# Weight sums of a two-level product: accumulating DMAs replaced by adds on GpSimd

## The chip, the cores and the metric

One core of a Trainium2 chip runs the whole program. The metric is the time of one execution on the device in microseconds (us). The kernel before takes 921.2 us (median of three executions, 921.12 to 921.84).

## What is computed

The reference chains three stages over 2304 tokens (4 batches of 576, model width 512).

```python
# 1. attention with exponential features (8 heads of 64)
proj = x @ w_phi; proj -= max(abs(proj)); phi = [exp(proj), exp(-proj)]
num = phi(q) @ (phi(k).T @ v);  den = phi(q) @ sum(phi(k));  x = num / (den + 1e-6)
# 2. mixture of 8 experts, each token to its best one
out[mask_e] = gate * (relu(x[mask_e] @ w1[e]) @ w2[e])
# 3. feed-forward
h = x @ w_in;  out = (h * sigmoid(h)) @ w_out        # w_in [512, 2048], w_out [2048, 512]
```

The weights `w_in` and `w_out` of stage 3 arrive as 64-bit floats, seen as pairs of 32-bit words; the kernel turns them into 32-bit floats itself.

## The kernel before, in words

**Precision.** TensorE multiplies in a reduced 32-bit format. To keep 32-bit accuracy nearly every operand x is split into a high part (a cast on ScalarE, ACT) and a low part (x minus the high part, on VectorE, DVE), and a product is three matmuls, high by high, low by high, high by low (`three`, lines 798 to 801).

**Three stretches.** Attention runs to about 230 us. From there to about 528 us come 22 expert "slots" of 128 tokens each, `for s in range(1, NSF + 1)` from line 1428. From 528 to 712 us run 32 "units" (`unit`, line 1112) that form h = x @ w_in, and after that w_out is applied (`down`, line 1176).

**A slot.** In the loop body for s, the first product of slot s (`mm1(s, k)`, k = 0 to 3) runs first, then the second product of slot s - 1 (`mm2(s - 1, i)`, i = 0 to 3). Behind each of these eight steps stand the splits of weights that are needed later (`split`, lines 848 and 849), the steps of the routing, and a call `convert(s, n)` with n = 0 to 7. `xturn` and `hturn` turn the inputs of the two products; their low parts `xl` and `hl` are made at line 856. The low part `hl` is the last thing that a second product waits for. PE, ACT, DVE, POOL (GpSimd) and SyncE (SP) each execute their instructions in the order in which this code writes them; in the units and after them POOL's own order is left to the framework.

**A unit.** Stage 3's first product is a seven-product scheme in place of eight: each pair q of 128-column blocks of w_in (eight pairs) gives seven weight matrices of 128x256. `unit(u)` goes through the products in the order 1, 5, 4, 6, 3, 2, 7, where 4 and 3 belong to the unit before; a plan `todo` hangs other work behind (unit, product). `keep` (line 1097, ACT) copies a partial sum from bank A out to an `ht` tile, `join` (line 1104, DVE) adds bank C or B to such a tile. Products 1, 6, 7, 4 accumulate in bank A, so each of them waits for the `keep` of the one before it; product 3 accumulates on product 5 in bank C, so it waits for the `join` of product 5. Products 1, 5, 2 of unit 0 and 1, 5 of unit 1 run ahead of the units, among the last slot's work.

**The seven weights.** A converted block holds two matrices of 128x256 (even block: A11 and A12, negated; odd block: A21, A22). The seven weights are these four, with one of them used alone in each place, and four sums. They are collected in HBM scratch, `sscr[q]`, seven places of 128x256. `keep_weights` (line 171) writes the four matrices, some of them to several places at once, and `add_weights` (line 191) then adds place n onto other places with a DMA that accumulates, HBM to HBM, issued by POOL. There are 21 such DMAs; `ADDS` and `WHEN` (lines 188, 189) put them into the slots, at the top of slot s, behind the gather of token rows for slot s + 2 (`gather`, line 834).

**Conversion.** Blocks 0 to 9 are converted on DVE during attention (`Convert`). Blocks 10 to 15 are converted in the slots (`cload`, `cwork`, `cstore`, lines 939 to 954): POOL issues the load of 512 KB, and `narrow` (line 197) takes four steps, one on ACT (line 202) and three on DVE (lines 209 or 212, 217, 219), in two raw buffers and one shared result buffer; an odd block also has one add on DVE (line 225). `HOOKS` (line 956) gives each block five places, the blocks lying in slots 4 to 8 and 13 to 16.

**Fetching.** `wfetch(q)` (line 984, SP) loads the seven places of pair q, 896 KB, straight into the buffer where the low parts will stand; `whigh` (line 990, ACT) casts them to the high parts, `wlow` (line 994, DVE) subtracts in place. Fetches of pairs 0 to 3 stand in slots 20 and 21, of 4 and 5 ahead of unit 0, of 6 and 7 in units 1 and 2. The 16 blocks of w_out are converted later, in units 6 to 24 (`oload`, `cwork`, `cstore`).

Of the kernel before, what the change touches and what calls it, by code (L numbers as in the profile page):

```python
# [49 lines left out]
RANK = (1, 0)  # L50
WARM = (10, 14)
# [15 lines left out]
def moe_kernel(ctx, tc, qk, v, w_phi, emb, tau, w1, w2, win, wout, out):  # L67
# [11 lines left out]
    sscr = [dram.tile([P, 7, 256], F32, name=f"sscr{i}") for i in range(NJP)]  # L79
# [91 lines left out]
    def keep_weights(i, c, rw, dma=nc.sync):  # L171
# [3 lines left out]
        if half:  # L175
            dma.dma_start(out=woscr[q][:, odd, :], in_=c)
        elif i < CA and odd:
            dma.dma_start(out=sscr[q][:, 6, :], in_=c[:, 0:256])
            dma.dma_start(out=sscr[q][:, 2:6, :], in_=c[:, 256:512].unsqueeze(1).to_broadcast([P, 4, 256]))
        elif odd:  # L180
            both = rw.rearrange("p f t -> p (f t)")[:, 0:256].bitcast(F32)
            dma.dma_start(out=sscr[q][:, 6, :], in_=c[:, 0:256])
# [5 lines left out]
    ADDS = [(q, n) for n in (6, 0, 1) for q in range(CA // 2)] + [(5, 0), (6, 0), (5, 1), (6, 1), (7, 0), (7, 1)]  # L188
    WHEN = [1, 1, 2, 2, 4, 6, 6, 6, 7, 7, 8, 13, 13, 13, 13, 14, 15, 15, 16, 17, 18]

    def add_weights(q, n):
        a, b = {6: (3, 6), 0: (4, 7), 1: (5, 6)}[n]
        src = sscr[q][:, n:n + 1, :]
        nc.gpsimd.dma_start(out=sscr[q][:, a:b, :], in_=src.to_broadcast([P, b - a, 256]) if b - a > 1 else src,
                            accum_op=ALU.add)

    def narrow(rw, c, eng, i):
        minus = i < NJ and i % 2 == 0
        lo, hi = rw[:, :, 0], rw[:, :, 1]
        def scale():  # L200
            if eng is nc.scalar:
                nc.scalar.mul(out=c.bitcast(F32), in_=hi.bitcast(F32), mul=2.0 ** -112)
            else:
                eng.tensor_scalar(out=c.bitcast(F32), in0=hi.bitcast(F32), scalar1=2.0 ** -112, scalar2=None,
                                  op0=ALU.mult)

# [20 lines left out]
    class Convert:  # L227
# [18 lines left out]
        def store(self, i):  # L246
            keep_weights(i, *self.h.pop(i))
# [1375 lines left out]
```

## Time and profile before

| | |
|---|---|
| median of 3 executions | 921.2 us (921.12 to 921.84) |
| profiled execution, its own time | 923.77 us |
| its span, first to last instruction | 922.1 us |
| granted TensorE clock in it | 0.998 of full speed |
| busy: PE, DVE, ACT, POOL | 901.1, 619.6, 581.9, 260.6 us |
| DMA in all | 171.69 MB; POOL's queue 26.55 MB of it |

The profile is of one execution; the sum of a prediction is made against its own time. PE is TensorE's matmuls; the end of a matmul is modelled, so two that follow each other overlap in the profile and a busy PE need not be at its peak. "Idle before <-X" names what released the instruction, by the profile. A group of instructions is named by its line of the kernel, its output and its inputs.

### The profile page before, as it was taken

The page shows a single profiled execution, that of the slowest core. Times are in us where ns is not written, and L with a number is a line of the kernel's source. Part 1 is how long each engine was busy: PE and PEld are TensorE (multiplying, and loading weights), DVE is VectorE, ACT ScalarE, POOL GpSimd, SP SyncE. Part 2 cuts the span into 40 slices and gives each one's busy share as a digit, 9 for nine tenths or more (in the row PEclk, how much of TensorE's full clock was granted, in tenths as well). Part 3 has the DMA queues.
Part 4 walks back from the last instruction along what each step waited for, and adds up shares of the span by engine and source line. Part 5 has one row for each costly group of instructions (what it writes and reads, how often), then busy time and mean ns, then how long its engine had stood idle before and what let it go on. Part 6 is the DMA issues. An engine that isn't in the chain of part 4 may idle for free. (4 is left out here: it accounts for less than half of the span.)

```text
span 922.1 us, 15645 instructions
## 1 busy us (share of the span) xinstructions
PE 901.1 (98%) x5567; PEld 786.3 (85%) x5567; DVE 619.6 (67%) x967; ACT 581.9 (63%) x948; POOL 260.6 (28%) x236
## 2 busy tenths in 40 slices
PE   8999999999999989999999999999999999999996
PEld 6999999988767767877888799999999888888885
DVE  7888888986798999969989857676756122222220
ACT  6877878745977869869888665343456344444331
POOL 6887877712221434313210020101000100000000
PEclk9999999999999999999999999999999999999999
DMA  6355363349496795793698585877776744444420
GB/s 181 107 152 180 93 178 97 99 126 359 160 256 194 237 240 170 277 322 110 180 335 305 196 289 180 248 248 231 242 255 210 202 115 125 115 114 115 116 67 23
DMA packets 136739, 171.69 MB, mean 186 GB/s; under 512 B 34664, under 2 KB 97768, under 8 KB 136656
## 3 DMA queue, kind: packets, MB, share of 16 engines
q1 hardware_dynamic: 124064, 144.06, 49.4%
q0 software_dynamic: 12512, 26.55, 10.8%
q8 instruction: 45, 0.74, 0.3%
q14 instruction: 38, 0.31, 0.1%
q10 hardware_dynamic: 80, 0.03, 0.0%
HBM read 170.87 MB, written 52.04 MB: 242 GB/s over the span
## 5 line engine op out<-in xcount | busy, mean ns | idle before, releaser
L849 DVE TENSOR_TENSOR wl<-raw,wh 128x1024 fp32r<-128x1024 f32 (+1 forms) x166 | 187.6, 1173 | 28.1 <-ACT wh L848 22.6
L848 ACT CAST wh<-raw 128x1024 fp32r<-128x1024 f32 (+1 forms) x166 | 161.2, 1033 | 22.2 <-PE ph L801 10.8
L1173 DVE TENSOR_TENSOR hlt<-gt,hlt 128x1024 fp32r<-128x1024 f32 x34 | 41.7, 1226 | 146.4 <-ACT hlt L1172 146.4
L1097 ACT COPY ht<-puA 128x288 f32<-128x288 f32 x128 | 50.9, 400 | 91.9 <-PE puA L801 78.9
L800 PE MATMUL po<-wob,hlt 128*128 128x512 f32 x272 | 108.6, 399 | 0.0
L799 PE MATMUL po<-wob,hlt 128*128 128x512 f32 x272 | 107.2, 394 | 0.0
L801 PE MATMUL po<-wob,hlt 128*128 128x512 f32 x272 | 106.6, 392 | 0.0
L435 POOL TENSOR_TENSOR kl<-ke,kh 128x640 fp32r<-128x640 f32 x52 | 84.0, 1636 | 31.0 <-issue 23.1
L1193 ACT COPY os<-po 128x512 f32<-128x512 f32 x17 | 10.0, 587 | 108.0 <-PE po L801 108.0
L485 PE MATMUL pnx<-kv,qp 128*128 128x73 f32 x640 | 76.6, 275 | 0.0
L485 PEld LDWEIGHTS pnx<-kv,qp 128*128 128x128 f32 x640 | 74.1, 192 | 0.1
L1194 POOL DMA_INDIRECT out<-os,oidx x18 | 17.5, 974 | 179.1 <-ACT os L1193 168.6
L799 PE MATMUL ph<-wh,xh 128*128 128x512 f32 x166 | 67.1, 404 | 0.0
L801 PE MATMUL ph<-wh,xl 128*128 128x512 f32 x166 | 65.3, 394 | 0.9 <-DVE xl L856 0.9
L800 PE MATMUL ph<-wl,xh 128*128 128x512 f32 x166 | 64.8, 390 | 0.0
L396 DVE TENSOR_REDUCE m<-pqk 128x10 f32<-128x1280 f32 x32 | 47.5, 1486 | 24.5 <-PE pqk L390 24.5
L1104 DVE TENSOR_TENSOR ht<-puC,ht 128x288 f32<-128x288 f32 x64 | 29.1, 454 | 51.4 <-PE puC L801 44.6
L799 PEld LDWEIGHTS po<-wob,hlt 128*128 128x128 f32 x272 | 51.1, 188 | 13.1
L420 ACT ACTIVATE ke<-d 128x640 f32<-128x640 f32 x52 | 38.3, 737 | 37.0 <-DVE d L397 37.0
L801 PEld LDWEIGHTS po<-wob,hlt 128*128 128x128 f32 x272 | 51.1, 188 | 12.3
L800 PEld LDWEIGHTS po<-wob,hlt 128*128 128x128 f32 x272 | 51.1, 188 | 11.8
L390 PE MATMUL pqk<-wbd,zh 128*128 128x256 f32 (+1 forms) x320 | 59.5, 285 | 0.8 <-DVE d L397 0.6
(403 smaller groups left out, 2438.3 us busy)
## 6 DMA issues: line engine op xcount, KB each, us to landing
raw<-w SPq DMA_DIRECT2D x44, 1536.0 KB
raw<-w SPq DMA_DIRECT2D x44, 512.0 KB
hd<-ht SPq DMA_DIRECT2D x124, 144.0 KB
gt<-hd SPq DMA_DIRECT2D x15, 1024.0 KB
z<-qk SPq DMA_DIRECT2D x32, 288.0 KB
wo<-wout SPq DMA_DIRECT2D x16, 512.0 KB
yd<-ys SPq DMA_DIRECT2D x23, 256.0 KB
raw<-win SPq DMA_DIRECT2D x10, 512.0 KB
```

What stands on the lines that cost most here:

```text
L390: nc.tensor.matmul(out=pqk[0:r, c * 256:(c + 1) * 256], lhsT=z[:, c * P:c * P + r], rhs=wbd[:, j].rearrange("p h f -> p (h f)"), start=(i ...
L396: nc.vector.tensor_reduce(out=m, in_=pv, axis=AX.X, op=ALU.max, apply_absolute_value=True)
L420: nc.scalar.activation(out=ke, in_=kd, func=AF.Exp, scale=1.0 - 2.0 * s)
L435: nc.gpsimd.tensor_tensor(out=kl[:, :, s, :], in0=st.pop(("ke", g, s)), in1=kh[:, :, s, :].bitcast(F32), op=ALU.subtract)
L485: nc.tensor.matmul(out=pn[:, c, 0:73], lhsT=qp[:, s, c * P:(c + 1) * P], rhs=kv[:, s, 0:73], start=(s == 0), stop=(s == 1))
L799: nc.tensor.matmul(out=o, lhsT=ah, rhs=bh, start=first, stop=False, skip_group_check=more)
L800: nc.tensor.matmul(out=o, lhsT=ah, rhs=bl, start=False, stop=False, skip_group_check=more)
L801: nc.tensor.matmul(out=o, lhsT=al, rhs=bh, start=False, stop=last, skip_group_check=more)
L848: nc.scalar.copy(out=hi[:, 0:n], in_=sl[:, 0:n])
L849: nc.vector.tensor_tensor(out=lo[:, 0:n], in0=sl[:, 0:n], in1=hi[:, 0:n].bitcast(F32), op=ALU.subtract)
L1097: nc.scalar.copy(out=htile(u, at), in_=BK[u, "A"])
L1173: nc.vector.tensor_tensor(out=lo, in0=g, in1=hi.bitcast(F32), op=ALU.subtract)
```

## The change

Pairs 0 to 2 are now converted in the slots, in place (`narrow_in_place`), and POOL forms their four sums right there (`csum`), in the parts of the raw buffers that the conversion has freed; `cstore` writes seven places. Pairs 3 to 7 are converted during attention and stored as four places; each is fetched into a staging tile (two of them in turn), POOL forms the four sums in the tile (`wsum`), and `whigh` and `wlow` read it from there. The places of conversion steps, of some unit tasks (`xscale`, `xsum` of T4, `wlow` of pair 2), of the `join` of product 5 and of the conversion of w_out move too.

```diff
-    def keep_weights(i, c, rw, dma=nc.sync):
+    def keep_weights(i, c, dma=nc.sync):
...
         elif odd:
-            both = rw.rearrange("p f t -> p (f t)")[:, 0:256].bitcast(F32)
-            dma.dma_start(out=sscr[q][:, 6, :], in_=c[:, 0:256])
-            dma.dma_start(out=sscr[q][:, 2, :], in_=c[:, 256:512])
-            dma.dma_start(out=sscr[q][:, 3:6, :], in_=both.unsqueeze(1).to_broadcast([P, 3, 256]))
+            dma.dma_start(out=sscr[q][:, 0, :], in_=c[:, 0:256])
+            dma.dma_start(out=sscr[q][:, 3, :], in_=c[:, 256:512])
         else:
-            dma.dma_start(out=sscr[q][:, 0:2, :], in_=c.rearrange("p (a f) -> p a f", a=2))
-    def add_weights(q, n):
...
+            dma.dma_start(out=sscr[q][:, 1:3, :], in_=c.rearrange("p (a f) -> p a f", a=2))
+    def narrow_in_place(flat, i):
+        rw = flat.rearrange("p (f t) -> p f t", t=2)
+        lo, hi = rw[:, :, 0], rw[:, :, 1]
+        shift(lo, i)
+        yield
+        nc.vector.scalar_tensor_tensor(out=lo, in0=hi, scalar=-2147483648, in1=lo, op0=ALU.bitwise_and,
+                                       op1=ALU.bitwise_xor)
+        yield
+        nc.scalar.mul(out=hi.bitcast(F32), in_=hi.bitcast(F32), mul=2.0 ** -112)
+        yield
+        c = flat[:, 0:512]
+        nc.vector.scalar_tensor_tensor(out=c, in0=hi, scalar=3, in1=lo, op0=ALU.logical_shift_left, op1=ALU.bitwise_or)
...
+        def csum(q):
+            a, b = J[2 * q][0], J[2 * q + 1][0]
+            a11, a12, s1, s2, a21, a22, s4, s3 = (x[:, o:o + 256] for x in (a, b) for o in range(0, 1024, 256))
+            for o, x, y in ((s1, a22, a21), (s3, a11, a21), (s2, s1, a11), (s4, s2, a12)):
+                nc.gpsimd.tensor_tensor(out=o, in0=x, in1=y, op=ALU.add)
+
+        def cstore(q):
+            for i, o, at in ((0, 0, 0), (0, 512, 3), (1, 512, 5)):
+                nc.gpsimd.dma_start(out=sscr[q][:, at:at + 2, :],
+                                    in_=J[2 * q + i][0][:, o:o + 512].rearrange("p (a f) -> p a f", a=2))
+            nc.gpsimd.dma_start(out=sscr[q][:, 2, :], in_=J[2 * q + 1][0][:, 256:512])
+
+        SLOTWORK = {(5, 7): (csum, 0), (6, 1): (cstore, 0), (7, 1): (cload, 2), (7, 3): (cload, 3),
+                    (11, 1): (csum, 1), (13, 1): (cstore, 1), (13, 5): (cload, 4), (13, 7): (cload, 5),
+                    (16, 1): (csum, 2), (16, 3): (cstore, 2)}
+        STEPS = [(2, 1), (2, 3), (2, 5), (2, 7), (4, 1), (4, 5), (5, 1), (5, 5)]
+        STEPS += [(s, n) for s in (9, 10, 14, 15) for n in (1, 3, 5, 7)]
...
+            else:
+                W["r", q] = pools["ul"].tile([P, 2048], F32, tag="ws", name="ws", bufs=2)
+                nc.sync.dma_start(out=W["r", q][:, 0:1024], in_=sscr[q].rearrange("p a f -> p (a f)"))
+
+        def wsum(q):
+            r = W["r", q].rearrange("p (a f) -> p a f", a=8)
+            for o, a, b in ((4, 3, 0), (7, 1, 0), (5, 4, 1), (6, 5, 2)):
+                nc.gpsimd.tensor_tensor(out=r[:, o], in0=r[:, a], in1=r[:, b], op=ALU.add)
...
-                if n == 5 and v >= 0:
+                if n == 1 and v >= 0:
                     join(v, 5)
...
             if s < NSF:
                 if s + 2 < NSF:
                     gather(s + 2)
-                for i, when in enumerate(WHEN):
-                    if when == s:
-                        add_weights(*ADDS[i])
...
             if s == NSF - 1:
                 xfetch(1, 0)
                 xfetch(1, 1)
-                wfetch(3)
...
+        wfetch(3)
+        wfetch(4)
...
-            for q in range(2, NJP):
-                at(q - 2, 6, whigh, q)
-                at(q - 1, 5, wlow, q)
-            at(1, 4, wfetch, 6)
-            at(2, 4, wfetch, 7)
+            for q, steps in {2: (None, None, (0, 6), (0, 3)), 3: (None, (0, 7), (1, 6), (2, 1)),
+                             4: (None, (1, 2), (2, 6), (3, 1)), 5: ((2, 5), (3, 1), (3, 7), (4, 5)),
+                             6: ((3, 6), (4, 4), (4, 7), (5, 5)), 7: ((4, 3), (5, 4), (5, 7), (6, 5))}.items():
+                for f, when in zip((wfetch, wsum, whigh, wlow), steps):
+                    if when:
+                        at(*when, f, q)
+            at(0, 2, xscale, 1, 0)
+            at(1, 2, xscale, 1, 1)
...
-                at(u + 6, 2, xsum, k, "T4")
+                at(u + 7, 1, xsum, k, "T4")
...
-            units = [u for u in range(6, 25) if u not in (7, 15, 23)]
+            units = [u for u in range(8, 26) if u not in (15, 23)]
```

## Rows read from the trace of the kernel before

**Rows 1.** The page, busy time, share of the span and instructions of each engine.

```profile
PE 901.1 (98%) x5567; PEld 786.3 (85%) x5567; DVE 619.6 (67%) x967; ACT 581.9 (63%) x948; POOL 260.6 (28%) x236
```

**Rows 2.** PE's waits, whole run: who waited for whom, us, times, longest.

```profile
PE po L801 <- DVE hl L856: 3.0, 3, 1.3
PE py L801 <- DVE hl L856: 1.8, 1, 1.8
PE puA L799 <- ACT ht L1097: 1.3, 2, 0.8
...
PE puC L799 <- DVE ht L1104: 0.6, 1, 0.6
```

**Rows 3.** Windows by stretch: length, busy us of each engine, clock, DMA share, GB/s.

```profile
323.00:353.00 30.00, 26.85 (x145) 20.91 (x144) 28.43 (x42) 21.07 (x32) 9.56 (x11) 1.00 0.88 221
...
402.00:416.00 14.00, 13.78 (x68) 10.77 (x67) 7.26 (x10) 8.11 (x14) 0.00 (x0) 1.00 0.88 289
416.00:429.00 13.00, 12.55 (x60) 9.81 (x59) 13.00 (x16) 13.00 (x19) 2.09 (x3) 1.00 0.30 98
```

**Rows 4.** PE's timeline at two waits: start, length, instruction [idle before <-releaser].

```profile
331.96 0.50 PE L801 MATMUL py<-wh,hl 128*128 128x512 f32 x1 [1.77 <-DVE hl L856]
...
346.41 0.51 PE L801 MATMUL po<-wh,hl 128*128 128x512 f32 x1 [1.33 <-DVE hl L856]
```

**Rows 5.** DVE's conversion steps in the slots: busy us, mean ns, idle before.

```profile
L217 DVE SCALAR_TENSOR_TENSOR x<-x 128x512 int32<-128x512 int32 x6 | 5.0, 826 | 0.0
...
L209 DVE TENSOR_SCALAR x<-x 128x512 int32<-128x512 int32 x3 | 1.3, 427 | 0.0
L225 DVE TENSOR_TENSOR x<-x 128x256 f32<-128x256 f32 x3 | 1.3, 424 | 0.0
```

**Rows 6.** ACT's timeline, two long idles in the slots.

```profile
341.69 0.66 ACT L202 ACTIVATE x<-x 128x512 f32<-128x512 f32 x1 [4.21 <-DMA sscr<-x]
...
407.89 0.62 ACT L848 CAST wh<-raw 128x512 fp32r<-128x512 f32 x1 [6.20 <-PE ph L801]
```

**Rows 7.** Accumulating DMAs from 380 to 402 us: issue ns, starts, issue to landing.

```profile
L194 POOL DMA_DIRECT2D sscr<-sscr x5: 1012/1410/1841, 385.4 to 398.0; - x5
...
DMA to landing us min/median/max: 8.1/10.4/11.6
```

**Rows 8.** DVE during attention: ns min/median/max of two lines.

```profile
L219 DVE SCALAR_TENSOR_TENSOR raw<-raw x10: 693/2062/2074, 29.9 to 192.0; 128x512 int32<-128x512 int32 x10
...
L397 DVE TENSOR_TENSOR d<-pqk,m x32: 1491/1492/1493, 9.7 to 220.2; 128x1280 f32<-128x1280 f32 x32
```

**Rows 9.** POOL's smallest two-input operation on 32-bit floats: busy us, mean ns.

```profile
L412 POOL TENSOR_TENSOR vl<-ve,vh 128x320 fp32r<-128x320 f32 x24 | 21.3, 887 | 0.9 <-ACT vh L409 0.9
```

**Rows 10.** ACT's timeline at the first units: pair 2's cast, then two copies.

```profile
530.41 1.69 ACT L990 CAST wb<-wb 128x1792 fp32r<-128x1792 f32 x1
532.00 0.70 ACT L1097 COPY ht<-puA 128x288 f32<-128x288 f32 x2
```

**Rows 11.** DVE's timeline there: pair 2's low part, a join, a scaling of tokens.

```profile
532.81 2.02 DVE L994 TENSOR_TENSOR wb<-wb 128x1792 fp32r<-128x1792 f32 x1
...
536.02 0.46 DVE L1104 TENSOR_TENSOR ht<-puB,ht 128x288 f32<-128x288 f32 x1 [0.41 <-PE puB L801]
536.40 0.48 DVE L1014 TENSOR_SCALAR yt<-yt,gate_s 128x512 f32<-128x512 f32 x1
```

**Rows 12.** PE's timeline there: first matmuls of product 3, unit 0, and of the next.

```profile
534.15 0.30 PE L799 MATMUL puC<-xcB,wb 128*128 128x288 f32 x1
...
534.95 0.30 PE L799 MATMUL puB<-xcB,wb 128*128 128x288 f32 x1
```

**Rows 13.** The DMA queue's timeline on SP: the fetch of pair 4.

```profile
528.96 0.47 SPq L987 DMA_DIRECT2D wbr<-sscr  x1
```

**Rows 14.** The chain of waits: start, us; a 512 KB load on SP's queue, a matmul.

```profile
602.69 5.17 DMA wo<-wout
...
712.16 0.23 PE po L799
```

More of the change, by code (lines that the diff above doesn't have):

```diff
@@ L78, in moe_kernel @@
     yd = dram.tile([NT + 2 * P, DM], F32, name="yd")
-    sscr = [dram.tile([P, 7, 256], F32, name=f"sscr{i}") for i in range(NJP)]
+    sscr = [dram.tile([P, 7 if i < QD else 4, 256], F32, name=f"sscr{i}") for i in range(NJP)]
     woscr = [dram.tile([P, 2, DM], F32, name=f"woscr{i}") for i in range(NJP)]
@@ L188, in moe_kernel @@
-    ADDS = [(q, n) for n in (6, 0, 1) for q in range(CA // 2)] + [(5, 0), (6, 0), (5, 1), (6, 1), (7, 0), (7, 1)]
-    WHEN = [1, 1, 2, 2, 4, 6, 6, 6, 7, 7, 8, 13, 13, 13, 13, 14, 15, 15, 16, 17, 18]
-    def add_weights(q, n):
[L192 to L198, printed above, removed]
-        lo, hi = rw[:, :, 0], rw[:, :, 1]
[L200 to L205, printed above, removed]
-        def shift():
-            if minus:
-                nc.vector.tensor_scalar(out=lo, in0=lo, scalar1=29, scalar2=-2147483648, op0=ALU.logical_shift_right,
-                                        op1=ALU.bitwise_or)
-            else:
-                nc.vector.tensor_scalar(out=lo, in0=lo, scalar1=29, scalar2=None, op0=ALU.logical_shift_right)
-        for f in (shift, scale) if eng is nc.scalar else (scale, shift):
-            f()
-            yield
@@ L972, in phase_all, with owork, ostore @@
+        def owork(j):
+            next(J[NJ + j][1], None)
+        def ostore(j):
+            keep_weights(NJ + j, J.pop(NJ + j)[0])
         J = {}
@@ L979, in wspace, with wside, wsource @@
         def wspace(q):
[L980 to L982 removed]
+            if q < 4:
+                wb = big.tile([P, 2, 2048], F32R, tag="blk", name="wb")
+                W[q] = wb[:, 0, 0:7 * 256], wb[:, 1, 0:7 * 256]
+            else:
+                W[q] = [wside(q, i) for i in range(2)]
+        def wside(q, i, dt=F32R):
+            return pools["ur"].tile([P, 7 * 256], dt, tag=f"wb{q}{i}", name="wbr", bufs=1)
         def wfetch(q):
[L985 removed]
+            if q < QD:
                 wspace(q)
[L987 removed]
+                nc.sync.dma_start(out=W[q][1].bitcast(F32), in_=sscr[q].rearrange("p a f -> p (a f)"))
+            else:
+                W["r", q] = pools["ul"].tile([P, 2048], F32, tag="ws", name="ws", bufs=2)
[4 more added lines that the diff above has]
+                nc.gpsimd.tensor_tensor(out=r[:, o], in0=r[:, a], in1=r[:, b], op=ALU.add)
+        def wsource(q):
+            return W["r", q][:, 256:] if q >= QD else W[q][1].bitcast(F32)
         def whigh(q):
[L990 removed]
+            if q not in W:
+                wspace(q)
+            nc.scalar.copy(out=W[q][0], in_=wsource(q))
         def wlow(q):
             hi, lo = W[q]
[L994 removed]
+            if lo is None:
+                lo = W[q][1] = wside(q, 1)
+            nc.vector.tensor_tensor(out=lo, in0=wsource(q), in1=hi.bitcast(F32), op=ALU.subtract)
         def tiles_of(k):
```

96 lines of the change are left out of this document (38 added, 58 removed).

## The prediction

> **What bounds the kernel now.** I read the page first: PE is busy for 98% of the span [rows 1], so the change can win little more than PE's idle time. The waits of PE say where that is [rows 2]: in the slots it waits for `hl`, the last low part that DVE makes for a second product, four times and 4.8 us in all; in the first units twice, 1.3 us, for ACT's copy out of bank A; later once, 0.6 us, for a join on DVE. The windows by stretch then put the slot waits in place [rows 3]. From 323 to 353 us (slots 7 and 8) PE is idle for 30.00 - 26.85 = 3.15 us while DVE is busy for 28.43 of 30: DVE is the limit. From 402 to 416 us neither DVE (7.26 of 14) nor ACT (8.11) is full; both wait for data, and DVE then works without a gap to 429 us. PE loses 0.22 + 0.45 us there. (The last of the four waits for `hl`, 1.2 us, lies at the end of slot 21, behind fetches of pairs 1 and 2 that do not change.) The timeline of PE gives the two large waits of slots 7 and 8, 1.77 and 1.33 us [rows 4]. A matmul of 512 columns takes a step of 0.23 us in the chain of waits [rows 14], but is shown for some 0.4 (108.6 us for 272 in the page's groups), so each wait costs about 0.17 us more than its idle row says.
>
> Around this kernel 0.2% (1.8 us) is about what a measurement can tell from no change.
>
> **The change, part by part.**
>
> *Attention (up to 230 us).* The same ten conversions; SP stores fewer copies of each odd block. DVE, ACT and POOL do the same work, and no PE wait in rows 2 names these stores. I take 0.
>
> *DVE's conversion in the slots.* A block costs DVE 0.43 + 0.69 + 0.69 = 1.8 us, and an odd block 0.42 more for its add [rows 5, 8] (0.69 is the undisturbed length of line 219; line 217's mean holds one instance that was held up). The three adds go. The steps move: from slots 4 to 8 and 13 to 16 into 2, 4, 5, 9, 10, 14, 15. Slots 6, 7 and 8 then hold no step, where there were about 1.8 + 1.8 + 0.4 + 0.7 us of them. Slots 7 and 8 are where the two waits of rows 4 lie.
>
> *The shared result buffer.* In slot 8 ACT sat idle for 4.21 us until a store of block 11 had landed, since block 12 writes the same buffer; the 1.33 us wait of PE follows 4.7 us later [rows 4, 6]. In place, that wait is gone. With it and with the steps out of slots 7 and 8 I count the second wait as gone: 1.33 + 0.17 = **-1.5 us**. The first one (1.77) has DVE work of slots 4 to 6 behind it. There the change takes out 3.6 us of DVE steps up to that point, puts 1.8 back, and adds what POOL's sums cost DVE, next; I leave it as it is.
>
> *The sums on POOL in the slots.* Twelve adds of 128x256. POOL has no row for that size; the nearest is 887 ns for 128x320 [rows 9], so an add takes between 0.71 (in proportion) and 0.89 us; I take 0.74, since part of the 887 does not grow with size. What does it cost DVE? During attention line 219, with two inputs in SBUF, takes 2.06 us in the median against 0.69 at the least, while line 397, which reads PSUM, does not vary at all [rows 8]. So a DVE instruction with two SBUF inputs waits until a running POOL operation ends, up to its whole length. The bounds for four adds are 0 (they fall on instructions that read PSUM) and 4 x 0.89 = 3.6 us; I take 1.7, because two of the four meet weight splits and the others mostly `hl` and `xl`, which read PSUM. For pair 0 that falls into slots 5 and 6, as much as the 1.8 us saved: hence no change at the first wait. Pairs 1 and 2 are summed in slots 11 and 16, which hold no step, where no wait of rows 2 lies: 0. Behind `csum` on POOL stand the gathers; each is written at the top of slot s for slot s + 2, more than a slot ahead of its use, so 3 to 5 us more on POOL hide; if that cover were gone PE would wait for its input transposes by as much.
>
> *The accumulating DMAs.* 21 go. Five were issued from 385 to 398 us and took 10.4 us to land in the median [rows 7], in one queue with a conversion's load, beside the loads of expert weights. In the middle of that ACT sat idle for 6.20 us before the cast of the last quarter of `w2` [rows 6]; the row names PE, which was long done, so I read it as the weights' load. Without these DMAs (384 KB each, read twice and written once) I expect the load in time: 0.22 + 0.45 us and 0.17 for each of three waits, **-1.1 us**. The new stores and loads on POOL's queue there (0.9 + 1.0 MB) move less than half as much.
>
> *First units, `wlow` of pair 2.* It moves from behind the `join` of product 5 to ahead of it. DVE runs in order: `wlow` waits for ACT's cast, which ends at 530.41 + 1.69 = 532.10 [rows 10], and takes 2.02 us, to 534.1; then come the join of product 2 (0.4), the scaling of a token tile (0.48), now also here, and only then the join of product 5 (0.46) [rows 11], done at about 535.5. Product 3 of unit 0 accumulates in the same bank and started at 534.15 [rows 12]. So PE waits 1.35 us: **+1.4 us**. The bounds are 0 (if ACT's cast comes earlier) and 2.1 (if POOL's first add also holds the scaling).
>
> *First units, the staging tiles.* The fetch of pair 3 leaves slot 21 and is issued where pair 4's was, at 528.96 [rows 13], behind SP's last store of slot output. A 512 KB load took 5.17 us in the units [rows 14], so it lands at about 534.1. Four adds (3.0 us, behind `wlow` 2 at first) end near 537.2. ACT's cast of pair 3 (1.69) waits for that, and the copy of product 7 of unit 1 stands behind it, done at about 537.2 + 1.7 + 0.35 = 539.25 [rows 10]. Product 4 of unit 1 needs it; it comes five products of 0.80 and four transposes after product 3 of unit 0, so not before 534.15 + 4.0 = 538.15 [rows 12], and 1.4 later with the term above, at 539.5: covered, 0. For pairs 5, 6 and 7 the cast moves from behind product 6 to behind product 7, so the copy of the next unit's product 1 comes 1.7 us after it and product 6 is due about then: 0.1 to 0.3 us each, **+0.5 us**. The twenty POOL adds hold DVE's low parts but not its joins, which read PSUM like line 397 [rows 8], and it is the joins that PE waits for: 0 otherwise.
>
> *Later units.* The join of product 5 moves one product (0.8 us) earlier and a sum of tokens away from it; the wait of 0.6 us [rows 2] falls to about 0.1: **-0.6 us** with the 0.17. The conversion of w_out starts two units later and ends one later, still ahead of the fetch that needs it: 0.
>
> Sum: -1.5 - 1.1 + 1.4 + 0.5 - 0.6 = **-1.3 us**. The profiled execution took 923.77, its span is 922.1; carried to the median of 921.2 this gives 919.9.
>
> **The rivals.**
>
> 1. *Fuller relief (918.0 to 916.1).* `wlow` 2 and the later casts cost nothing, because the casts and joins find gaps: -3.2 us, 918.0. If the first wait of slot 7 goes as well (1.77 + 0.17), 916.1. For it speaks that DVE is the one limit there [rows 3] and that removed work there counts in full; against it, that the order on DVE at 532 us follows from the code.
>
> 2. *The staging chain comes late (923.9, slower).* One mechanism: fetch, four adds, cast, in a row, for each of pairs 3 to 7, with two tiles in turn. Pair 7 has about 8.2 us from the place of its fetch to the place of its cast (ten products of 0.80) [rows 12]. With 5.17 us to land [rows 14], 3.0 for the adds and up to 2.0 behind a `wlow` on DVE [rows 8, 11] it needs 10.2. ACT then stands still, the copies behind it are late, and PE waits, once the lateness passes about 1.2 us. Price: 2.4 for pair 3 if its load lands 2.5 us later than I assume, 0.8 for pair 6 and 0.8 for pair 7: 919.9 + 4.0 = 923.9. Against it: a load can land faster in the first units, where fewer transfers compete.
>
> 3. *POOL's adds take DVE's relief back (921.5).* Each add blocks DVE for its whole length and the 12 fall on splits. At 0.74 us each that is 3.0 us for pair 0, 1.3 more than I take, at a place without slack (+1.3), and 0.3 in slots 11 and 16. For it: line 219 above. The Trainium skill (SBUF — State Buffer, section Who interferes with whom) has this as a rule: a DVE instruction with two SBUF inputs and a GpSimd instruction that reads SBUF exclude each other for a whole instruction; rows 8 agree, and by it alone this rival would be the forecast for the slots.
>
> 4. *The weights were late for another reason (921.0).* Then removing the accumulating DMAs does not bring the load at 408 us forward, and the 1.1 us stay.
>
> **How the numbers follow.** The forecast has 0.38 (own range 918.4 to 921.4; a third of it below 919.4), rival 1 0.27, rival 2 0.21, rival 3 0.08, rival 4 0.06. Faster by over 0.2% (below 919.4): 0.12 + 0.27 + a little of 3 and 4 = 0.41. Slower (above 923.0): rival 2 and the top of the forecast's bounds, 0.22. The same: 0.37. The range runs from 916.1, the end of rival 1, to 923.7, within rival 2.
>
> **What would show it.** Right: PE's wait near 346 us is gone while one near 332 us stays; from 402 to 429 us ACT has no idle of several us; at 534 us PE waits about 1.3 us for a join, behind `wlow` of 2.02 us; the 0.6 us wait for puC is gone. Wrong: a long DVE `hl` wait in slot 3 or slots 5 to 6 beyond 2 us (steps or POOL's adds too dense), ACT idle for POOL before the casts of pairs 3 to 7 with PE waits behind them (rival 2), or four splits each in slots 5, 11 and 16 that take some 0.7 us more than their neighbours (rival 3).

## The result and the profile after the change

The changed kernel takes 930.1 us in the median of four runs (927.83 to 930.19); the kernel before took 921.35 us in the median of its four runs on that chip (921.12 to 921.84). The ratio is 1.0088 (1.0071 to 1.0106): slower, where I had forecast 919.9 us. The profiled execution took 930.03 us with a span of 928.3, against 923.77 and 922.1.

The page of the changed kernel, busy time:

```profile
span 928.3 us, 15661 instructions
PE 901.6 (97%) x5567; PEld 787.5 (85%) x5567; DVE 624.8 (67%) x964; ACT 584.1 (63%) x948; POOL 267.9 (29%) x247
```

DVE and ACT are busier by 5.2 and 2.2 us than before [rows 1], POOL by 7.3, and PE's work is the same to 0.5 us. So the 6.3 us of span are PE's waits and the end of the span. PE's waits from 300 us on (who waited for whom: us in total, times, longest):

```profile
PE puA L788 <- ACT ht L1110: 4.7, 4, 2.7
PE puA L788 <- PEq L1582: 1.6, 1, 1.6
PE py L790 <- DVE hl L845: 1.2, 1, 1.2
PE puC L788 <- DVE ht L1117: 1.1, 1, 1.1
PE ph L790 <- DVE xl L845: 1.0, 1, 1.0
PE po L790 <- DVE hl L845: 0.6, 1, 0.6
```

The waits for `hl`, four times and 4.8 us before [rows 2], are down to two and 1.8 us. In their place stand waits of the units: ACT's copies (4.7 us, 1.3 before [rows 2]), PE's own sequencer, the part that branches, at line 1582 (1.6) and a join (1.1). Their places, from PE's timeline (start, length, [idle before <-releaser]):

```profile
311.57 0.50 PE L790 MATMUL ph<-wh,xl 128*128 128x512 f32 x1 [1.03 <-DVE xl L845]
332.39 0.50 PE L790 MATMUL py<-wh,hl 128*128 128x512 f32 x1 [1.23 <-DVE hl L845]
344.95 0.39 PE L790 MATMUL po<-wh,hl 128*128 128x512 f32 x1
531.44 0.40 PE L788 MATMUL puC<-xcB,wb 128*128 128x288 f32 x1 [1.14 <-DVE ht L1117]
554.91 0.37 PE L788 MATMUL puA<-xcA,wbr 128*128 128x288 f32 x1 [1.64 <-PEq L1582]
566.25 0.61 PE L788 MATMUL puA<-xcT2n,wbr 128*128 128x288 f32 x1 [2.72 <-ACT ht L1110]
692.49 0.40 PE L788 MATMUL puA<-xcT,wb 128*128 128x288 f32 x1 [0.66 <-ACT ht L1110]
```

The third row answers to the one of 346.41 us [rows 4]: its wait is gone. Setting the same matmul of both traces side by side shows where time came and went:

| matmul | before, us | after, us | after less before |
|---|---|---|---|
| slot 6, `xl` | 310.76 | 311.57 | +0.81 |
| slot 7, `hl` | 331.96 | 332.39 | +0.43 |
| slot 8, `hl` | 346.41 | 344.95 | -1.46 |
| 423 us, `hl` | 423.07 | 420.09 | -2.98 |
| end of slot 21, `hl` | 522.41 | 518.38 | -4.03 |
| unit 0, product 3 (join) | 534.15 | 531.44 | -2.71 |
| transposes ahead of unit 5 | 552.20 | 550.27 | -1.93 |
| first one behind the conditional | 555.34 | 554.91 | -0.43 |
| unit 6, product 6 | 563.78 | 566.25 | +2.47 |
| 1.6 us of work later | 565.36 | 569.30 | +3.94 |
| unit 13, product 3 (join) | 612.10 | 615.32 | +3.22 |
| unit 21, product 3 | 659.23 | 662.21 | +2.98 |
| behind the first casts of w_out, copy | 688.73 | 692.49 | +3.76 |
| last matmul | 914.67 | 918.77 | +4.11 |
| end of POOL's drain | 921.22 | 927.49 | +6.27 |

So the slots gained 4.0 us, more than the 2.6 that I had counted; the units then lost 8.1 and the end 2.2. In the stretch where the accumulating DMAs had held the weights, PE now works through (windows: length, busy us of each engine, clock, DMA share, GB/s; [rows 3] are those of before):

```profile
323.00:353.00 30.00, 28.77 (x156) 22.79 (x155) 29.83 (x40) 24.04 (x36) 12.89 (x10) 1.00 0.51 180
402.00:416.00 14.00, 14.00 (x67) 11.34 (x66) 10.12 (x11) 11.17 (x17) 1.89 (x1) 1.00 0.87 326
416.00:429.00 13.00, 13.00 (x63) 10.51 (x62) 12.67 (x16) 13.00 (x21) 1.47 (x1) 1.00 0.26 82
```

The largest loss is at 566 us. First POOL's timeline there, then ACT's:

```profile
559.16 0.95 POOL L1019 DMA_INDIRECT yt<-yd,yidx  x1 [6.39 <-PE puA L790]
560.13 4.05 POOL L993 TENSOR_TENSOR ws<-ws 128x256 f32<-128x256 f32 x4
...
564.21 1.68 ACT L1001 CAST wbr<-ws 128x1792 fp32r<-128x1792 f32 x1 [2.62 <-POOL ws L993]
565.80 0.69 ACT L1110 COPY ht<-puA 128x288 f32<-128x288 f32 x2
```

POOL's queue had a gather of tokens ahead of the sums of pair 7, and the gather waited 6.39 us for PE. The four adds came at 560.13, took 4.05 us, ACT's cast waited 2.62 us for them, and the copies that PE needed stood behind the cast. After this wait TensorE ran at the lower of its two levels, 1.2 GHz, for some 3 us (granted clock 0.50 in the third last column of the windows), and PE lost another 1.5 us:

```profile
566.00:567.00 1.00, 0.75 (x3) 0.75 (x4) 1.00 (x1) 0.50 (x2) 0.00 (x0) 0.51 0.88 238
567.00:569.00 2.00, 2.00 (x10) 2.00 (x9) 1.62 (x2) 0.40 (x1) 0.00 (x0) 0.50 0.23 82
```

Two losses lie on sequencers (PEldq and POOLq in the rows): PE's branch at the conditional (line 1582; 1567 before), and the longest of POOL's three drains at the very end (line 1634; 1619 before), behind which the kernel ends. Durations are ns, shortest/median/longest. Of the kernel before:

```profile
L1567 PEldq COMPARE_BRANCH  x1: 625/625/625, 553.5 to 553.5; - x1
...
L1619 POOLq DRAIN  x3: 51/109/5245, 916.0 to 921.8; - x3
```

and of the changed kernel:

```profile
L1582 PEldq COMPARE_BRANCH  x1: 3402/3402/3402, 551.3 to 551.3; - x1
...
L1634 POOLq DRAIN  x3: 51/109/7405, 920.1 to 928.0; - x3
```

The table explains 6.3 us, the medians differ by 8.8: the profiled execution of the kernel before, 923.77 us, was longer than any of its timed runs here. No trace of a shorter one exists, so the other 2.5 us are not placed. On the five chips of the experiments the kernel before has medians of 923.1 to 924.1 us, with single runs from 920.6 to 928.7, so a part of the 8.8 may lie in the four runs here and not in the change.

### The profile page after: what moved, and what is told of

Same layout as the page of the kernel before. It is cut to its first block, busy times and chain, and to the rows that moved or that the text cites. A ratio compares the mean times of both kernels' runs of the same rounds, so it can differ in the third digit from the quotient of the medians.

```text
span 928.3 us, 15661 instructions
## 1 busy us (share of the span) xinstructions
PE 901.6 (97%) x5567; PEld 787.5 (85%) x5567; DVE 624.8 (67%) x964; ACT 584.1 (63%) x948; POOL 267.9 (29%) x247
## 5 line engine op out<-in xcount | busy, mean ns | idle before, releaser
L838 DVE TENSOR_TENSOR wl<-raw,wh 128x1024 fp32r<-128x1024 f32 (+1 forms) x166 | 192.2, 1201 | 22.1 <-ACT wh L837 16.8
```

Source lines behind the costliest of these rows:

```text
L838: nc.vector.tensor_tensor(out=lo[:, 0:n], in0=sl[:, 0:n], in1=hi[:, 0:n].bitcast(F32), op=ALU.subtract)
```

## Experiments

The kernels of one group ran on one chip, beside their own runs of the kernel before. The chips differ by some us, so ratios are compared, and in a profile the places of the waits.

### POOL's order, the join, the accumulating DMAs, the sums on DVE (e1 to e4)

**e1** writes out POOL's order in the units (the engines in `ORDERED` keep the order of the code; `ET.Pool` adds POOL to them):

```diff
-        block.enter_context(tc.manual_schedule(engines=ORDERED))
+        block.enter_context(tc.manual_schedule(engines=ORDERED | {ET.Pool}))
         slots.close()
...
+        block.close()
+        block.enter_context(tc.manual_schedule(engines=ORDERED))
```

> Only POOL's order in the units changes: the gather of a token tile for the third group of units, which stood ahead of pair 7's four adds, now stands behind them. Theory (order): pair 7's fetch had landed by about 557.6 us and the adds waited 2.5 us behind that gather, which waited for PE's transposes; so ACT's cast of pair 7 comes 2.5 us earlier, PE's wait of 2.9 us near 566 us shrinks to under 0.5, TensorE's clock does not fall to half behind it (1.6 us), and the time falls by about 4 us, to 926. Rival (late data, or DVE holding the adds): the fetch and the adds themselves are late; then the wait stays at 2 us or more and the time falls by under 1.5 us.

Measured: 926.9 us, ratio 1.0030 (1.0014 to 1.0047), span 924.7. POOL's timeline has the gather behind the adds, and ACT's cast follows without a wait:

```profile
558.51 2.93 POOL L993 TENSOR_TENSOR ws<-ws 128x256 f32<-128x256 f32 x4 [5.83 <-SPq L1582]
561.60 1.30 POOL L1019 DMA_INDIRECT yt<-yd,yidx  x1 [0.15 <-issue]
...
561.99 1.69 ACT L1001 CAST wbr<-ws 128x1792 fp32r<-128x1792 f32 x1
```

PE's 2.88 us at 566 are gone and its clock stays at the upper level; everywhere else PE's steps differ from those of the changed kernel by 0.35 us or less. That queue order is the largest single cause: 3.6 us of span. The adds end 2.7 us earlier than in the changed kernel: 1.6 because no gather stands ahead of them, and 1.1 because they take 2.93 us instead of 4.05, with less of DVE's work beside them. The branch (2.15 us in PE's steps), the wait near 690 us (1.08) and the drain (7.41) stay.

**e2** puts the low part of pair 2 back behind product 5 of unit 1 (the changed kernel otherwise):

```diff
-            for q, steps in {2: (None, None, (0, 6), (0, 3)), 3: (None, (0, 7), (1, 6), (2, 1)),
+            for q, steps in {2: (None, None, (0, 6), (1, 5)), 3: (None, (0, 7), (1, 6), (2, 1)),
```

> Only the low part of pair 2 goes back behind the join of product 5 of unit 0. Theory: PE's 1.1 us wait for that join near 531 us (1.3 from start to start) goes, and 1.3 us of time with it, 928.8. Rival: DVE then makes pair 2's low part later and unit 2 waits for it, or the later stall of pair 7 simply grows by as much, and the time stays at 930.

Measured: 928.05 us, 1.0045 (1.0028 to 1.0062). The join's wait goes, and 4 us later PE waits as long for ACT, whose cast of pair 3 waited 2.98 us for POOL's sums:

```profile
535.52 0.40 PE L788 MATMUL puA<-xcT,wb 128*128 128x288 f32 x1 [1.03 <-ACT ht L1110]
```

My term of 1.4 us is real, but undoing it alone wins nothing at that place: the cast is the next in line. The span is 926.1 us all the same, 2.2 less than the changed kernel's: the wait near 566 us was 1.78 us from start to start instead of 2.88, and the clock did not fall behind it. Why that wait was shorter was not tested.

**e3** is the kernel before without its 21 accumulating DMAs (the sums are left out):

```diff
-                for i, when in enumerate(WHEN):
-                    if when == s:
-                        add_weights(*ADDS[i])
```

> The kernel before without its 21 accumulating DMAs (the four sums of each pair are left out), all else as it was. Theory: the waits of PE for hl from 402 to 429 us go (1.1 to 1.5 us) with ACT's idle of 6.2 us, as the load of weights is in time; the waits near 332 and 346 us shrink by under 1 us, since they are DVE's work and the shared buffer; time 919.5 to 920.2. Rival: these DMAs are not what makes the weights late, and the time stays within 0.5 us of before. Besides: POOL's last drain took 5.2 us before and 7.4 in the changed kernel; if that follows from the number of POOL's DMAs (96 and 75), it is 7.4 here too and costs 2.2 us; if not, 5.2.

Measured: 920.98 us, 0.9973 (0.9961 to 0.9985). Its waits of PE from 300 us on:

```profile
PE py L801 <- DVE hl L856: 1.5, 1, 1.5
PE puA L799 <- ACT ht L1097: 1.3, 2, 0.8
PE po L801 <- DVE hl L856: 0.8, 1, 0.8
```

The last matmul comes 5.1 us earlier than in the kernel before: 4.3 of it by the end of slot 21, much as in the changed kernel (4.0). So what the DMAs cost in the slots, the change does get back. But the drain grew here too, to 7.41 us.

Two waits went that I had put down to something else. At 346 us PE waits 0.14 us instead of 1.33, where I had expected less than 1 us of change: ACT's step on the shared result buffer, which stood idle for 4.21 us in the kernel before [rows 6], comes without a wait, though the buffer is still shared:

```profile
337.13 0.73 ACT L202 ACTIVATE x<-x 128x512 f32<-128x512 f32 x1
```

The store that it had waited for was late when these DMAs were there. And the wait for the join at 612 us is gone with the join at its old place. In the kernel before, a conversion step of w_out that DVE had ahead of this join waited for its load:

```profile
607.89 0.43 DVE L204 TENSOR_SCALAR wo<-wo 128x512 f32<-128x512 f32 x1 [0.68 <-DMA wo<-wout]
...
612.10 0.40 PE L799 MATMUL puC<-xcB,wbr 128*128 128x288 f32 x1 [0.62 <-DVE ht L1104]
```

In e3 and in the changed kernel the same step starts without a wait.

**e4** has the sums of the units on DVE:

```diff
-                nc.gpsimd.tensor_tensor(out=r[:, o], in0=r[:, a], in1=r[:, b], op=ALU.add)
+                nc.vector.tensor_tensor(out=r[:, o], in0=r[:, a], in1=r[:, b], op=ALU.add)
```

> The twenty adds in the units go from POOL to DVE, in the same places of the program. Theory: four adds take 4 x 0.42 = 1.7 us of DVE in place of 3 to 4.6 us of POOL, they wait for no gather, and ACT's cast of pair 7 is in time: the 2.9 us wait and the slow clock behind it go (-4 us). Against it: DVE waits in order for each fetch (5 us from issue to landing) and holds the joins up, up to 1 us per pair at PE: +2 to +4. I expect 927 to 930. The rival, that DVE's order makes it worse than POOL, gives over 931.

Measured: 926.58 us, 1.0026 (1.0007 to 1.0046). The wait at 566 us is gone without any word on POOL's order, but the join's grows from 1.30 to 2.66 us, since the four adds of pair 3 now stand ahead of it on DVE too. That price, 1.4 us, is below the 2 to 4 that I had expected.

### The store of w_out, the drain, the sums in the slots, the place of the branch (e5 to e8)

**e5** is e1 with the conversion of w_out a unit earlier:

```diff
-            units = [u for u in range(8, 26) if u not in (15, 23)]
+            units = [u for u in range(7, 25) if u not in (15, 23)]
```

> The changed kernel with POOL's order in the units written out (as in e1_pool_order) and, besides, every w_out conversion one unit earlier (units 7 to 24 without 15 and 23, instead of 8 to 25). Theory: PE's last wait near 689 to 692 us (0.8 to 1.1 us) is for the first fetch of the converted w_out, which SP issues only behind the store of the last converted block; with the store one unit earlier that fetch is issued in unit 26 some 6 us sooner, the wait goes, and the span is 0.8 to 1.1 us under e1's (about 923.7 us, ratio to before 1.0015 to 1.003). Rival: the fetch is late for its own transfer (the queue is full of other fetches), then the wait stays and the span with it. Price to watch: a conversion in unit 7 meets the sums and casts of pair 7, which could push unit 7 or 8 by up to 1 us.

Measured: 926.67 us, 1.0032 (1.0020 to 1.0044): no gain. The wait near 690 us is gone, so its cause was the one named, SP's queue. In the changed kernel, the store of the last block, the fetch behind it, and ACT's cast that waits for the fetch:

```profile
684.86 0.38 SPq L177 DMA_DIRECT2D woscr<-wo  x1
685.34 0.41 SPq L1123 DMA_DIRECT2D hd<-ht  x1
685.80 0.45 SPq L1152 DMA_DIRECT2D wob<-woscr  x1
...
690.79 1.05 ACT L1155 CAST wob<-wob 128x1024 fp32r<-128x1024 f32 x1 [2.51 <-DMA wob<-woscr]
```

But the conversion's steps now meet the low parts of the tokens on DVE, and PE waits 0.94 us for a join at 578 us. In the profiled execution, 927.72 us, PE also lost 1.9 us between 555 and 562 us, where its clock was granted 0.50 for some 3 us.

**e6** adds 21 DMAs of 256 bytes on POOL's queue to e5:

```diff
+    junk = dram.tile([24, 64], F32, name="junk")
...
+            if s in (12, 17, 18) and n < 7:
+                k = (12, 17, 18).index(s) * 7 + n
+                nc.gpsimd.dma_start(out=junk[k:k + 1, :], in_=emb[0:1, 0:64])
```

> e5_pool_store plus 21 DMAs of 256 bytes on POOL's queue, in slots 12, 17 and 18, where POOL is idle most of the time; POOL then issues 96 DMAs as in the kernel before, not 75. The drain that POOL runs at the end of the kernel took 5.25 us before and 7.41 us in every kernel with 75 POOL DMAs. Theory: the length goes by how many DMAs POOL has issued, so with 96 the drain is 5.25 us again and the span is 2.2 us under e5's. Rival: it goes by what the 21 accumulating DMAs moved or by the accumulation, not by their number; then the drain stays at 7.4 us and the span equals e5's, or is up to 1 us over it where the small DMAs delay a gather.

Measured: 929.2 us, 1.0057 (1.0039 to 1.0076). The drain is longer, not shorter:

```profile
L1640 POOLq DRAIN  x3: 51/109/9124, 917.1 to 926.8; - x3
```

So 21 small DMAs more make the drain longer, (9.124 - 7.405) / 21 = 0.082 us for each, and the theory's 5.25 us falls: the kernel before has 96 DMAs on POOL's queue too, but something in it shortens the drain.

**e7** leaves out POOL's sums in the slots. (Here and in e9, e11, e13 and e14 the expectations say pair 5, or pairs 5 to 7, for what the slots convert. So it was in the kernel before; in the changed kernel these are pairs 0 to 2.)

```diff
         def csum(q):
             a, b = J[2 * q][0], J[2 * q + 1][0]
+            return
```

> The changed kernel without POOL's four sums in slots 5, 11 and 16; the stores write what the buffers hold (sums of pairs 5, 6 and 7 left out). Theory: the wait of about 1 us for xl at 311 us, which the kernel before doesn't have, comes from DVE's split being held by POOL's sums, so it is gone (under 0.2 us) and PE runs 0.8 us ahead of the changed kernel up to slot 9; the rest as in the changed kernel. Rival: the wait comes from the conversion steps that moved to slot 5, then it stays at about 1 us.

Measured: one run, 929.3 us. PE's wait for `xl` at 311 us is as long as with the sums (1.16 us between starts against 1.20). The rival holds, and the trace of the changed kernel could have said so: there the first sums in the slots start at 315.65 us, behind the wait. At 332 us PE is no earlier either: it then waits 1.4 us for ACT's `hh`.

**e8** is e5 with the conditional a unit earlier:

```diff
-            if u == NJP - 3:
+            if u == NJP - 4:
```

> e5_pool_store with the conditional (the If around the rest of the routing) ahead of unit 4 instead of unit 5. In the kernel before PE lost 0.3 us there, in the changed kernel 1.8, in e1 2.15, because the branch waits until its target's code has been fetched. Theory: the loss goes by how early PE's queue reaches the branch against that fetch, so at another place it is another number between 0.3 and 2.2 us; nothing in the rows says which. Rival: the loss comes from the data of that place (a value that the branch compares, read from the routing's result), then it is about 2 us here too.

Measured: 929.8 us, 1.0060 (1.0038 to 1.0082); PE loses 3.05 us at the branch. The two expectations overlap at 2 us and this is beyond both, so the run speaks for the first only weakly.

### Steps, casts, POOL's DMAs, the conditional (e9 to e12)

**e9**, from e1:

```diff
-        STEPS = [(2, 1), (2, 3), (2, 5), (2, 7), (4, 1), (4, 5), (5, 1), (5, 5)]
+        STEPS = [(2, 1), (2, 3), (2, 5), (2, 7), (3, 1), (3, 5), (4, 5), (5, 1)]
```

> e1_pool_order with the four conversion steps of the second tile of pair 5 moved from slot 4 positions 1 and 5 and slot 5 positions 1 and 5 to slot 3 positions 1 and 5, slot 4 position 5 and slot 5 position 1, so that ScalarE has its step at position 5 of slot 4 and VectorE one at position 1 of slot 5, as in the kernel before. Theory: the wait of about 1 us for xl at 311 us is the price of the step order (a VectorE step of 1.5 us that went to the second half of slot 4 delays the gate chain of the routing and with it the split); it goes (under 0.2 us), and PE runs 0.8 us ahead of e1 from there on: span about 923.9 us, ratio to before 1.001 to 1.003. Rival: the wait comes with any VectorE work in slots 3 to 5 and only moves there: then the span is e1's (924.7 us).

Measured: 930.43 us, 1.0070 (1.0056 to 1.0085). Both expectations fall: the wait at 311 us grew to 2.35 us between starts, and PE lost more at 334 and 411 us.

**e10**, from e9, with the low part of pair 2 as in e2 and the cast and the low part of pair 3 later:

```diff
+            for q, steps in {2: (None, None, (0, 6), (1, 5)), 3: (None, (0, 7), (1, 7), (2, 5)),
```

> e9_slot_steps with, besides, the remainder of pair 2's weights (2.0 us on VectorE) after product 5 of unit 1 as in the kernel before, the cast of pair 3 after product 7 of unit 1 instead of product 6, and its remainder after product 5 of unit 2 instead of product 1. Theory: in e2_join_first the wait of 1.2 us at 535 us was ScalarE's copies behind a cast that itself waited 3 us for POOL's sums of pair 3; behind product 7 the cast has its sums (they are ready at 533.4 us) and no copy of unit 1 stands behind it: of the 1.30 us that PE lost for the join at 531 us at least 0.8 go, span 0.8 to 1.3 us under e9's. Rival: the cast is then late for unit 3 or its 1.7 us stand ahead of unit 2's first copy, and PE waits there 0.5 to 1.3 us instead: span as e9's.

Measured: 930.3 us, 1.0067 (1.0048 to 1.0085), as e9. The join's 1.3 us go; 0.39 and 0.76 us of waits for ACT's copies come in unit 2 and ahead of unit 4. The rival holds.

**e11**, from e9, with POOL's loads and stores of the conversion on SP (the stores of pairs 0 and 2 also stand a few steps later):

```diff
-            fetch_raw(i, flat.rearrange("p (f t) -> p f t", t=2), nc.gpsimd)
+            fetch_raw(i, flat.rearrange("p (f t) -> p f t", t=2))
...
-                nc.gpsimd.dma_start(out=sscr[q][:, at:at + 2, :],
+                nc.sync.dma_start(out=sscr[q][:, at:at + 2, :],
```

> e9_slot_steps with POOL's six fetches and twelve stores of w_in pairs 5 to 7 on SP's queue (the stores of pair 5 at position 5 of slot 6, those of pair 7 at position 1 of slot 17), so that POOL issues 57 DMAs instead of 75. e6 had 21 more and a drain of 9.12 us for 7.41: 0.082 us for each. Theory: the drain goes by the number of POOL's DMAs: 7.41 less 18 x 0.082 = 5.9 us, and the span is 1.5 us under e9's. Rival: only DMAs after some point in the run count (the kernel before, with 96, had 5.25): then the drain can be anything from 2 to 7.4 us. Price to watch: SP waits in order, so a store that waits for a sum could hold the weight fetches of slots 6 to 17 (a wait of PE for wh or wl there).

Measured: 927.1 us, 1.0040 (1.0021 to 1.0059). The span, 925.4 us, is 3.7 us under e9's, more than the theory's 1.5; the rest came in the slots, where PE waits 0.45 us at 333 us and not 1.62. The drain took 5.94 us, where 5.9 had been worked out from e6:

```profile
L1636 POOLq DRAIN  x3: 40/113/5940, 918.6 to 925.1; - x3
```

**e12** is e9 without the conditional:

```diff
-                more = nc.values_load(regs[0:1, 2, NSF:NSF + 1], min_val=0, max_val=NT + P)
-                with tc.If(more < NT + P):
-                    rest()
```

> e9_slot_steps without the conditional ahead of unit 5 (the rest of the routing, which these inputs do not enter, left out). Theory: the 2.0 to 2.2 us that PE loses there in the changed kernel are on the path: the span is 2 us under e9's. In the kernel before the same place cost 0.31 us. Rival: the units behind are held by something else (POOL's gathers, the cast of pair 7) and the time comes back as another wait: span within 0.5 us of e9's.

Measured: 928.45 us, 1.0064 (1.0044 to 1.0083); the interval overlaps e9's. The branch's wait is gone, and with it 1.78 us against e9. A new wait of 1.20 us for ACT's copies at 566 us gives 1.0 of them back. Theory and rival each have about half. (By 556 us PE is 3.7 us ahead of e9, but 1.9 of them arose ahead of the branch, where the two kernels are the same.)

### What is left of the loss (e13 to e18)

**e13** is e1 with e11's queue change alone.

> e1_pool_order with POOL's six fetches and twelve stores of pairs 5 to 7 on SP's queue (as in e11, but the conversion steps at the change's own places). Theory: the drain is 5.94 us as in e11 (7.41 in e1), and VectorE is held less in slots 6 and 7, since POOL issues no stores there: the wait at 332 us falls from 1.3 to 0.6 us or less; span 1.5 to 2.5 us under e1's 924.7, ratio to before 1.000 to 1.0015. Rival: only the drain changes: span 1.5 us under e1's.

Measured: 924.41 us, 1.0009 (0.9995 to 1.0022). The drain is 5.94 us and the slots are as in e1 (1.36 us between starts at 332 us, 1.33 in e1): at that place it makes no difference who issues, though between e9 and e11 the wait there did shrink. The rival holds: only the drain changes. (The profiled execution is the longest of twelve, 927.69 us, with 3 us at the lower clock level.)

**e14**, from e13, converts the two blocks of pair 0 in slots 4 to 5 and 6 instead of 2 and 4 to 5; their sums, their stores and the next loads move behind them:

```diff
-        STEPS = [(2, 1), (2, 3), (2, 5), (2, 7), (4, 1), (4, 5), (5, 1), (5, 5)]
+        STEPS = [(4, 1), (4, 5), (5, 1), (5, 5), (6, 1), (6, 3), (6, 5), (6, 7)]
```

> e13 with pair 5's first tile converted in slots 4 and 5 (as in the kernel before) and its second in slot 6 instead of slots 2 and 4 to 5; the sums then in slot 7, the next fetches in slot 8. Theory: VectorE's routing steps in slots 2 to 5 have one tile's steps beside them, not two, and run 1.2 us earlier: the wait for xl at 311 us (1.0 to 1.2 us) goes. The steps in slot 6 bring back part of the kernel before's wait at 332 us (1.77 us): span 0 to 1 us under e13's. Rival: the wait at 311 us stays, then its cause is in the routing or the loads, not in the conversions.

Measured: 924.18 us, 1.0007 (0.9995 to 1.0018), span 922.2: level with the kernel before. PE's waits from 300 us on:

```profile
PE puA L788 <- ACT ht L1110: 2.0, 3, 0.8
PE puA L788 <- PEq L1582: 1.9, 1, 1.9
PE py L790 <- DVE hl L845: 1.3, 1, 1.3
PE puC L788 <- DVE ht L1117: 1.1, 1, 1.1
PE po L790 <- DVE hl L845: 1.0, 1, 1.0
PE ph L790 <- DVE xl L845: 0.7, 1, 0.7
```

The `xl` wait at 311 us is gone (the 0.7 is at 338 us): it came from the steps of two blocks beside the routing on DVE in slots 2 to 5. The same reduction of the routing starts at 302.68 us here and at 304.32 in the changed kernel. But PE reaches the last `hl` of slot 21 at 518.29 us, in the changed kernel at 518.38: those 0.8 us were no loss by the end of the slots.

**e15** and **e16** are e13 and e14 with e4's sums on DVE.

> e13 with the sums of pairs 3 to 7 in the units on VectorE instead of POOL (as in e4). Theory: e4's units ended 1.0 us ahead of e1's at the same slots (the branch 0.5 instead of 2.15 us, the join 2.7 instead of 1.3): span 0.5 to 1 us under e13's. Rival: the branch's loss comes and goes with the place of the instruction fetch and the join's 1.4 us are then the whole difference: span 1.4 us over e13's.

> e14 with the sums of pairs 3 to 7 on VectorE: all that was found to help, in one kernel. Theory: span as e14's less 0.5 to 1 us, ratio to before 0.997 to 1.000, so as fast as the kernel before or up to 0.3% faster. Rival: as for e15, then ratio 1.000 to 1.002.

Measured: 925.91 us, 1.0020 (1.0008 to 1.0032), and 924.71 us, 1.0014 (1.0001 to 1.0026). The branch costs 0.57 and 0.73 us instead of 2.0, the join 2.65 instead of 1.29. The rivals hold: no gain over POOL.

**e17** and **e18** are e14 with the conditional ahead of units 3 and 2 (`NJP - 5`, `NJP - 6` in e8's line).

> e14_slots_4_and_6 with the conditional ahead of unit 3 (about 540 us) instead of unit 5. Theory: the branch ends 2.4 to 2.6 us after a fetch of PE's code starts; the regular fetch of this stretch starts at about 533 us, 7 us ahead of the branch here, so if that fetch holds the branch's target PE loses 0.3 us or less, the span is 1.7 us under e14's 922.2 and the ratio to before 0.998 to 1.000. Rival: the target lies beyond what the regular fetch holds and a fetch of its own starts at the branch: then PE loses 2 to 3 us as at units 4 and 5 and the span is e14's or up to 1 us over it.

> e14_slots_4_and_6 with the conditional ahead of unit 2 (about 533 us), close to the regular fetch of PE's code at 533 us. Theory: as in the kernel before, where the fetch started 1.8 us ahead of the branch, PE loses 0.3 to 1 us; span 1 to 1.7 us under e14's. Rival: a fetch of its own as at units 4 and 5, 2 to 3 us; span e14's or up to 1 us over it.

Measured: 927.87 us, 1.0046 (1.0030 to 1.0062), and 925.57 us, 1.0023 (1.0012 to 1.0034). In e18 PE loses 2.34 us, as the rival had it. In e17 the branch is short, and three us of code later PE stands still for no semaphore:

```profile
L1582 PEldq COMPARE_BRANCH  x1: 352/352/352, 538.7 to 538.7; - x1
...
546.02 0.29 PE L789 MATMUL puA<-xcT2n,wb 128*128 128x288 f32 x1 [2.62 <-issue]
```

A fetch of PE's code starts at 543.12 us there, and PE goes on 2.9 us later. The wait was put off, not saved. No version that does all the work beat the kernel before; e13 and e14 equal it within their intervals.

## Why the prediction was wrong

The sum of -1.3 us was made of waits that engines impose on each other, read where the change adds or removes work. Nearly all of these sizes came out, two of them (at 346 and at 612 us) not for the reason that I gave. What failed is **the sentence that the twenty POOL adds cost "0 otherwise"**: I asked whom they hold on DVE, and not what stands ahead of them in POOL's own queue. Three more places had no price: the branch and POOL's drain had no term, and the store that SP's queue holds ahead of the w_out fetch stood as "still ahead of the fetch: 0".

- *Attention, 0.* Right: no matmul before 310 us is shifted by more than 0.35 us.
- *Slots 7 and 8, -1.5.* The second wait is gone and the first stays, 1.23 us for 1.77, as forecast; from 332 to 346 us PE gained 1.9. But the -1.5 for the second wait is right by luck as far as its reason goes: I put it down to the shared buffer and to DVE's steps, and e3, which keeps both, wins 1.2 of it by leaving out the accumulating DMAs. The sharing cost something only while the store was late. The price ahead of it, the new `xl` wait of 0.81 us at 311 us, I had not seen: I counted the steps of slots 4 to 6, and those that move into slot 2 fall beside the routing on DVE. e14 shows the cause, and that it cost nothing in the end.
- *POOL's sums in the slots.* I took 0.74 us an add. The twelve took 0.73 at the least, 1.39 in the median and 1.73 at the most; DVE's weight splits ran beside them and took up to 1.77 us, where their median is 1.22. By the Trainium skill (SBUF — State Buffer, section Who interferes with whom) a DVE instruction with two SBUF inputs and a GpSimd instruction that reads SBUF exclude each other; the spread agrees. Against their undisturbed lengths four adds cost DVE 1.3 to 1.5 us, near the 1.7 that I took, and POOL about 2. PE got nothing back without them in the one run of e7: rival 3 falls.
- *The accumulating DMAs, -1.1.* Right in kind, too small: its own parts add up to 1.2, 402 to 429 us gave 1.5, and the wait at the end of slot 21, which I had left unchanged, another 0.6. By e3 all of them together cost PE 5.1 us, the 1.2 at 346 and 0.8 at 612 us among them. Rival 4 falls.
- *`wlow` of pair 2, +1.4.* Measured +1.3 at the place named, behind a `wlow` of 2.02 us. e2 and e10 add what I did not say: the copies behind the cast of pair 3 are due as late, so at that place the term can't be taken back alone.
- *Staging, 0 for pair 3 and +0.5 for pairs 5 to 7.* Right for pair 3. For pair 7 it cost 2.9 us and 1.5 more at the lower clock. That is the place and the wait of rival 2, ACT standing still for POOL, to which I gave 0.21; but its cause there, a slow load and adds held by DVE, was at most a part: against e1 the adds came 1.6 us later, behind the gather, and took 1.1 us longer. e1 changes the order alone and the wait is gone.
- *The join of product 5, -0.6.* The number came out, -0.7 at 612 us, but e3 loses the same wait with the join unmoved, so what made it was the late load of w_out; that the move did anything is not shown.
- *Without a term:* the branch +1.5, the w_out fetch +0.8, the drain +2.2, and a gather that came late for the transposes ahead of unit 5, +0.4.

Against the forecast of 919.9, the slots were 1.4 better, the units 6.8 and the end 2.2 worse; the remaining 2.5 are the difference between the profiled execution of the kernel before and its median, by which I had carried the sum over.

## What to carry to other kernels

When work moves to an engine that also issues DMAs, list its queue in order at each new place and ask what each entry ahead of the work waits for: here a gather that waited for PE cost some 4 us, and fixing the order got 3.6 of them back. A trace's waits price what is removed; they can't price a queue position that doesn't exist yet, so every instruction put into a queue needs its neighbours read from the code. And look at both ends of the span: eighteen DMAs, moved to another queue, were worth 1.5 us in a drain that no engine's busy time shows. Last, a wait that goes as forecast does not yet show its reason: e3, which changes one thing, took two of my reasons away.

## What the runs showed of the hardware

- **POOL's last drain grows with the number of its DMAs**: 5.94 us with 57, 7.41 with 75, 9.12 with 96, which is 0.081 and 0.082 us for each. The kernel before has 96 too and 5.25 us; 21 of them accumulate. Why those shorten the drain is open.
- **A branch ends behind a fetch of code.** In every trace with this branch the profile's instruction queue shows a fetch of 16 KB near it, and except in e17 the branch ended 2.3 to 3.0 us after that fetch began. That the fetch is PE's, and the cause, is read from these times alone. In the kernel before the fetch began 1.8 us ahead of the branch and it took 0.63 us; in the changed kernel 1.0 us behind it, and it took 3.40. What sets the start of the fetch is not settled; moving the branch (e8, e17, e18) only moved the price. The Trainium skill (Advanced Engine Details and Errata, section Control Flow Timing) gives about 108 ns for a compare-and-branch; PE's took more in every run here, 0.35 us at the least (e17) and 4.4 at the most (e8).
- **TensorE's clock can fall after a wait**: after 2.9 us of waiting it was granted 0.50 for some 3 us, which cost 1.5 us. Waits of 2.0 and 3.1 us in e5 and e8 were followed by a stretch at that level too, those of 2.2 us in e1 and e6 and of 2.8 us in e17 were not; what decides it, the rows don't say.
